# Turning z one pair before it is rounded, with a second buffer, in a fused attention and two-network kernel

## The chip, the core and the metric

The kernel runs on one core of a Trainium2 chip. The metric is the device time of one execution in microseconds (us), as a median over runs. Five engines have in-order queues of their own: TensorE (PE, with its weight loads as PEld), VectorE (DVE), ScalarE (ACT), GpSimd (POOL) and SyncE (SP, which here issues nearly all DMAs).

## The reference

```python
scores = matmul(z, z.T) / S          # z: (2, 3008, 64)
attn = maximum(scores, 0) ** 2
x = u * matmul(attn, v)              # u, v: (2, 3008, 256)
x = x.reshape(6016, 256)
h = x @ w_in1                        # w_in: (256, 2048), w_out: (2048, 256)
x = (h - tanh(h)) @ w_out1
h = x @ w_in2
g = where(h >= 1, h, where(h <= -1, 0, (h + 1) ** 2 / 4))
out = g @ w_out2
```

## The kernel before, in words

Each fp32 operand of a product is split in two rounded parts, `hi` (a ScalarE copy to the rounded type) and `lo` (VectorE: the operand less `hi`), and a product is three matmuls.

The program is one list of *pairs*, `pairs`. An attention pair is a batch b, a chunk c of 512 queries (six per batch, the last of 448) and two key tiles t of 128; there are twelve t. The first half of a pair, `attn_s`, makes the scores (six matmuls), the relu `r` (ScalarE, line 271), `hi` (line 274), the squares `a` (VectorE line 280; for every third t ScalarE line 278) and `lo` (VectorE, line 284, queued at the end of the pair). The second half, `attn_av`, accumulates `hi` and `lo` times v, and runs LAG = 2 pairs later. At a chunk's last pair two accumulators are added to `y` (lines 320, 321). A network pair is a chunk of 512 tokens and 256 hidden columns, done likewise (`ffn_s`, `ffn_av`, 24 matmuls). The score tiles and h have two PSUM buffers.

In the first chunk of each batch z (six tiles of 512 columns per batch), v (twelve) and, in the first chunk of each network, the weights (sixteen) are brought in *loads*. A load is a list of steps, each with the number of pairs by which it stands at the latest before its first use. The first is the DMA to a tile of the pool `raw` (six buffers), issued on SP's queue; then comes the work that puts the split operand into a ring of 18 tiles. For z the work is `turn` (VectorE transposes the raw tile into `zt`, line 126) and `cut` (ScalarE rounds `zt`, line 131; VectorE subtracts, line 132). For v and the weights it is a split (line 90 on ScalarE, line 93 on VectorE, where VectorE's part is put off to the next `flush`). `pump(i)` runs at the head of each pair i: it starts loads, does the steps that are due, and may do one more step ahead of time for a load whose last step lies two pairs back. Here `zt` has one buffer, and turn and cut of z are one step, `work`. A pool hands a buffer on in the order in which the program frees it.

The weights come as 8-byte numbers; a generator `convert` turns them with VectorE instructions spread over the attention pairs, and writes them back to memory. The pool `wide` (two buffers) holds their raw form. At the start, while the first DMAs are under way, `warm` runs matmuls on a tile `zero`.

Of the kernel before, what the change touches and what calls it, by code (L numbers as in the profile page):

```python
# [9 lines left out]
U32 = mybir.dt.uint32  # L10
BF16 = mybir.dt.bfloat16
# [4 lines left out]
P = 128  # L16
# [4 lines left out]
AHEAD = 14  # L21
# [6 lines left out]
def attention_then_two_ffn(  # L28
# [29 lines left out]
    const = ctx.enter_context(tc.tile_pool(name="const", bufs=1))  # L58
# [3 lines left out]
    wide_p = ctx.enter_context(tc.tile_pool(name="wide", bufs=2))  # L62
    raw_p = ctx.enter_context(tc.tile_pool(name="raw", bufs=6))
    u_p = ctx.enter_context(tc.tile_pool(name="u", bufs=2))
    zt_p = ctx.enter_context(tc.tile_pool(name="zt", bufs=1))
    tmp_p = ctx.enter_context(tc.tile_pool(name="tmp", bufs=2))
    sp_p = ctx.enter_context(tc.tile_pool(name="split", bufs=3))
    ps_s = ctx.enter_context(tc.tile_pool(name="ps_s", bufs=2, space=bass.MemoryType.PSUM))
# [9 lines left out]
    loads = []  # L78
    deferred = []

    def add_load(first, last, steps, slots=1):
        loads.append({"first": first, "last": last, "steps": steps[:2], "slots": slots, "parts": steps[2:]})

    def flush():
        for fn in deferred:
            fn()
        deferred.clear()
# [15 lines left out]
    def load_z(b, g):  # L103


        st = {}

        def dma(other=nc.sync):
            r = st["raw"] = raw_p.tile([P, QT], F32, tag="raw", name=f"zraw{b}_{g}")
            r3 = r.rearrange("p (c e) -> p c e", e=32)  # L110
            n = min(QT, S - QT * g) // 32
            for i in range(4):
                d = slice(32 * (i % 2), 32 * (i % 2) + 32)
                at = slice(32 * i, 32 * i + 32)
                (other if i % 2 else nc.sync).dma_start(
                    out=r3[at, :n, :],
                    in_=z[b, QT * g : QT * g + 32 * n, d].rearrange("(c a) e -> a c e", a=32),
                )
                if 32 * n < QT:
                    nc.sync.dma_start(  # L120
                        out=r3[at, n:, :], in_=z[b, S - REST :, d].rearrange("(c a) e -> a c e", a=32)
                    )

        def turn():
            st["zt"] = zt_p.tile([P, QT], F32, tag="zt", name=f"zt{b}_{g}")
            nc.vector.transpose(out=st["zt"], in_=st["raw"])  # L126

        def cut():
            zt = st["zt"]
            w = ring.tile([P, 2, QT], F32R, tag="w", name=f"z{b}_{g}")  # L130
            nc.scalar.activation(out=w[:, 0, :], in_=zt, func=AF.Copy, scale=ZEXP)
            nc.vector.scalar_tensor_tensor(
                out=w[:, 1, :], in0=zt, scalar=ZEXP, in1=w[:, 0, :].bitcast(F32), op0=ALU.mult, op1=ALU.subtract
            )
            zs[b, g] = w

        def work():
            turn()
            cut()

        return [(dma, AHEAD), (work, 2), turn, cut]

    def load_v(b, t):

# [309 lines left out]
    pairs = []  # L454
# [6 lines left out]
    for b in range(B):  # L461
        base = len(pairs)
        end = base + QC * NPA - 1
        lastc = base + (QC - 1) * NPA
        for t in range(NPA):
            if t % 2 == 0:
                g = t // 2

                add_load(base + t, end if g == QC - 1 else lastc + t + 1, load_z(b, g))
            add_load(base + t + LAG, lastc + t + LAG, load_v(b, t))  # L470
        for c in range(QC):
            p0 = len(pairs)
            for j in range(4):
                hook(p0 + UL + j, load_u, b, c, j)
            hook(p0 + UT, turn_u, b, c)
            for t in range(NPA):
                pairs.append((attn_s, attn_av, (b, c, t)))
    for net, (wi, wo) in enumerate(((w_in1, w_out1), (w_in2, w_out2))):
        base = len(pairs)
        for f in range(NPF):  # L480
            lastc = base + (NCH - 1) * NPF + f
            rows = slice(f * 2 * P, (f + 1) * 2 * P)
            cols = slice(f * 4 * P, (f + 1) * 4 * P)
            converts.append(convert((net, "in", f), wi[:, cols].rearrange("(k p) f -> p k f", p=P)))
            converts.append(convert((net, "out", f), wo[rows, :].rearrange("(k p) d -> p k d", p=P)))
            add_load(base + f, lastc, load_w((net, "in", f)))
            add_load(base + f + LAG, lastc + LAG, load_w((net, "out", f)))
        for c in range(NCH):
            hook(len(pairs) - 3, split_x, net, c)
            for f in range(NPF):  # L490
                pairs.append((ffn_s, ffn_av, (net, c, f)))

    zero = const.tile([P, 512], BF16, name="zero")

    def warm(n):

        ps = ps_a.tile([P, 512], F32, tag="acc", name="warm")
        for i in range(n):
            nc.tensor.matmul(ps, zero[:, :P], zero, start=True, stop=True)

    with tc.manual_schedule():
        nc.gpsimd.memset(zero, 0.0)

        live = []
        staged = []

        def advance(ld, i):
            ld["steps"].pop(0)[0]()
            ld["at"] = i
            if not ld["steps"]:  # L510
                staged.remove(ld)
                live.extend([ld["last"]] * ld["slots"])

        def pump(i):

            while loads and len(staged) < 4 and loads[0]["first"] <= i + AHEAD:
                ld = loads[0]
                free = RING - sum(x >= i - 1 for x in live) - sum(y["slots"] for y in staged)
                if free < ld["slots"]:
                    break  # L520
                loads.pop(0)
                staged.append(ld)
                advance(ld, i)
            n = 0
            for ld in list(staged):
                while ld in staged and ld["first"] - ld["steps"][0][1] <= i:
                    advance(ld, i)
                if i > 5 and ld in staged and ld["at"] < i - 1 and n < (i >= NATT or pairs[i][2][2] != 1):
                    advance(ld, i)
                    n += 1  # L530


        first = [loads.pop(0) for _ in range(4)]
        z0, v0, v1, z1 = first
        z0["steps"][0][0](nc.scalar)
        v0["steps"][0][0]()
        v1["steps"][0][0](nc.scalar)
        z1["steps"][0][0]()
        warm(WARM[0])
        z0["steps"][1][0]()  # L540
        v0["steps"][1][0]()
        flush()
        z1["parts"][0]()
        for ld in first:
            live.append(ld["last"])

        held = {}
        state = {"credit": 0.0, "step": 0}
        NATT = B * QC * NPA

        pauses = ((0, NPA), (NPA * QC - 9, NPA * QC + 13), (NATT - 5, NATT + 1))

        def make(i):

            if not any(a <= i < e for a, e in pauses):
                state["credit"] += CONVERT[0] if i < NATT else CONVERT[1]
            while converts and state["credit"] >= 1:
                state["credit"] -= 1
                state["step"] += 1
                if state["step"] == 1:  # L560
                    next(converts[0])
                elif state["step"] == 5 and len(converts) > 1:
                    next(converts[1])
                if next(converts[0], "end") == "end":
                    converts.pop(0)
                    state["step"] = 1

        def second(i):
            if i >= LAG:
                _, av_fn, args = pairs[i - LAG]  # L570
                av_fn(*args, *held.pop(i - LAG))

        def close():
            for fn in tail:
                fn()
            tail.clear()

        for i in range(len(pairs) + LAG):
            pump(i)
            for fn, args in hooks.get(i, ()):  # L580
                fn(*args)
            if i == LAG:
                second(i)
            if i < len(pairs):
                s_fn, _, args = pairs[i]
                held[i] = s_fn(*args)
            else:
                flush()
            if i == 0:
                close()  # L590
                z1["parts"][1]()
            elif i == 1:
                warm(WARM[1])
                close()
                v1["steps"][1][0]()
                flush()
            if i != LAG:
                second(i)
            make(i)
            close()  # L600
# [32 lines left out]
```

## Time and profile before

| what | value |
|---|---|
| median of 3 runs | 1536.03 us (1535.98 to 1537.39) |
| the profiled execution, its own time | 1536.36 us |
| its span in the trace | 1534.4 us |
| TensorE busy | 1519.9 us, 99% |
| VectorE busy | 1077.6 us, 70% |
| ScalarE busy | 818.9 us, 53% |

The span runs from the program's first instruction to its last; the execution's own time is 1.96 us longer. Every time stamp below is counted from the start of the span. Busy time of TensorE is modelled, and the matmuls are pipelined, so a late matmul is best seen by the distance of the starts. The attention lasts to about 500 us, the first network to about 1010 us.

### The profile page before, as it was taken

The numbers are of one execution on the slowest core, as the hardware profiler recorded it, in microseconds if no ns is written. First come the engines' busy times: TensorE is split into PE (matmuls) and PEld (weight loads), VectorE is DVE, ScalarE is ACT, GpSimd is POOL, SyncE is SP. The second block draws the span as 40 slices with busy tenths as digits, with TensorE's granted clock in tenths as the row PEclk, the third lists the DMA queues.
The fourth block names the chain that finished last, engine by engine and source line by source line (L and its number), as shares of the span: only waits on it lengthen the run. The fifth ranks groups of instructions, "written<-read, shape, count | busy, mean of one in ns | idle before, by whom it ended". The sixth has DMA issues, their size and how long they took to land.

```text
span 1534.4 us, 21242 instructions
## 1 busy us (share of the span) xinstructions
PE 1519.9 (99%) x8944; PEld 1264.8 (82%) x8944; DVE 1077.6 (70%) x1139; ACT 818.9 (53%) x866; POOL 0.7 (0%) x5
## 2 busy tenths in 40 slices
PE   9999999999999999999999999999999999999999
PEld 5788888888889888888888888897888888888888
DVE  7888887888888765666654444567767776777675
ACT  7777777877778544444444444454444444344443
POOL 0000000000000000000000000000000000000000
PEclk9999999999999999999999999999999999999999
DMA  6222143123224201110010000020000000000001
GB/s 136 65 56 56 49 102 66 32 56 80 53 56 109 76 21 41 42 41 25 25 49 0 0 1 1 14 55 14 1 14 14 15 14 15 14 14 4 11 15 25
DMA packets 146623, 56.69 MB, mean 37 GB/s; under 512 B 123616, under 2 KB 130144, under 8 KB 146528
## 3 DMA queue, kind: packets, MB, share of 16 engines
q1 hardware_dynamic: 145056, 54.81, 14.5%
q8 instruction: 70, 1.15, 0.3%
q10 hardware_dynamic: 1472, 0.52, 0.1%
q14 instruction: 25, 0.20, 0.0%
HBM read 40.76 MB, written 14.55 MB: 36 GB/s over the span
## 4 chain that ended last, share of the span: by engine, by line
PE 93%; DVE 4%; ACT 2%; issue 1%; DMA 1%; SPq 0%; DVEq 0%; ACTq 0%
PE acc L386 32%; PE acc L298 21%; PE h L355 11%; PE h L356 11%; PE h L354 11%; PE sc L263 5%; DVE a L280 1%; DVE lo L284 1%; PE acc L418 1%; ACT r L271 1%; DMA zraw<-in_z_dram 0%; DVE zt L126 0%; ACT hi L274 0%; DVE gl L93 0%; ACT a L278 0%
## 5 line engine op out<-in xcount | busy, mean ns | idle before, releaser
L386 PE MATMUL acc<-gh,w_out 128*128 128x512 f32 (+1 forms) x1472 | 360.3, 387 | 0.0
L90 ACT ACTIVATE gh<-g 128x1024 fp32r<-128x1024 f32 (+1 forms) x192 | 200.4, 1044 | 268.2 <-DVE g L373 142.5
L298 PE MATMUL acc<-hi,v 64*128 64x512 f32 (+1 forms) x2256 | 317.0, 385 | 5.4 <-DVE y L321 3.1
L386 PEld LDWEIGHTS acc<-gh,w_out 128*128 128x128 f32 x1472 | 275.5, 188 | 54.8
L355 PE MATMUL h<-xh,w_in 128*128 128x512 f32 (+1 forms) x768 | 295.7, 385 | 0.9 <-DVE w_in L93 0.7
L354 PE MATMUL h<-xl,w_in 128*128 128x512 f32 (+1 forms) x768 | 295.7, 385 | 0.0
L356 PE MATMUL h<-xh,w_in 128*128 128x512 f32 (+1 forms) x768 | 295.5, 385 | 0.0
L298 PEld LDWEIGHTS acc<-hi,v 64*128 64x128 f32 x2256 | 240.4, 184 | 52.0 <-DVE y L321 7.4
L93 DVE TENSOR_TENSOR gl<-g,gh 128x1024 fp32r<-128x1024 f32 (+1 forms) x192 | 230.0, 1198 | 68.6 <-ACT gh L90 68.6
L365 DVE TENSOR_TENSOR g<-h,t 128x1024 f32<-128x1024 f32 (+1 forms) x96 | 115.4, 1202 | 148.2 <-ACT t L363 148.2
L368 DVE TENSOR_SCALAR t<-h 128x1024 f32<-128x1024 f32 (+1 forms) x96 | 115.4, 1203 | 142.6 <-PE h L356 142.6
L284 DVE TENSOR_TENSOR lo<-a,hi 128x1024 fp32r<-128x1024 f32 (+1 forms) x144 | 172.7, 1200 | 53.7 <-ACT a L278 52.4
L386 PE MATMUL acc<-gl,w_out 128*128 128x512 f32 (+1 forms) x736 | 195.0, 387 | 0.0
L298 PE MATMUL acc<-lo,v 64*128 64x512 f32 (+1 forms) x1152 | 189.4, 384 | 1.7 <-DVE lo L284 1.5
L271 ACT ACTIVATE r<-sc 128x1024 f32<-128x1024 f32 (+1 forms) x144 | 144.9, 1006 | 85.6 <-PE sc L263 83.4
L371 ACT ACTIVATE t<-t 128x1024 f32<-128x1024 f32 (+1 forms) x96 | 100.3, 1044 | 156.8 <-DVE t L368 156.8
L363 ACT ACTIVATE t<-h 128x1024 f32<-128x1024 f32 (+1 forms) x96 | 96.9, 1009 | 160.8 <-PE h L356 160.7
L355 PEld LDWEIGHTS h<-xh,w_in 128*128 128x128 f32 x768 | 144.1, 188 | 29.6 <-DVE w_in L93 2.2
L354 PEld LDWEIGHTS h<-xl,w_in 128*128 128x128 f32 x768 | 144.2, 188 | 28.3 <-issue 0.9
L356 PEld LDWEIGHTS h<-xh,w_in 128*128 128x128 f32 x768 | 144.2, 188 | 27.6
L386 PEld LDWEIGHTS acc<-gl,w_out 128*128 128x128 f32 x736 | 137.8, 188 | 27.5
L298 PEld LDWEIGHTS acc<-lo,v 64*128 64x128 f32 x1152 | 137.2, 184 | 22.9 <-DVE lo L284 3.8
(54 smaller groups left out, 1098.2 us busy)
## 6 DMA issues: line engine op xcount, KB each, us to landing
wide_in<-in_moe_w_in_dram SPq DMA_DIRECT2D x16, 512.0 KB, 4.2
wide_out<-in_moe_w_out_dram SPq DMA_DIRECT2D x16, 512.0 KB, 3.9
out_dram<-ot SPq DMA_DIRECT2D x88, 64.0 KB, 1.9
vraw<-in_v_dram SPq DMA_DIRECT2D x21, 256.0 KB, 3.1
ub<-in_u_dram SPq DMA_DIRECT2D x80, 64.0 KB, 2.7
w_in<-m_in SPq DMA_DIRECT2D x16, 256.0 KB, 2.2
w_out<-m_out SPq DMA_DIRECT2D x16, 256.0 KB, 2.2
wraw_in<-w_in SPq DMA_DIRECT2D x16, 256.0 KB, 2.8
```

The costliest lines, as they stand in the source:

```text
L90: nc.scalar.activation(out=hi, in_=src, func=AF.Copy)
L93: nc.vector.tensor_tensor(out=lo, in0=src, in1=hi.bitcast(F32), op=ALU.subtract)
L271: nc.scalar.activation(out=r[s], in_=ps[s], func=AF.Relu)
L284: tail.append(lambda: nc.vector.tensor_tensor(out=lo[s], in0=a[s], in1=hi.bitcast(F32)[s], op=ALU.subtract))
L298: nc.tensor.matmul(acc[d][h][:, :n], lhsT, g[half, j, :n], start=start, stop=stop)
L354: nc.tensor.matmul(ps[:, j, :n], w[:, 0, k, fs], xl[:, k, :n], start=(k == 0), stop=False)
L355: nc.tensor.matmul(ps[:, j, :n], w[:, 1, k, fs], xh[:, k, :n], start=False, stop=False)
L356: nc.tensor.matmul(ps[:, j, :n], w[:, 0, k, fs], xh[:, k, :n], start=False, stop=(k == 1))
L365: nc.vector.tensor_tensor(out=g[s], in0=ps[s], in1=t1[s], op=ALU.subtract)
L368: nc.vector.tensor_scalar(out=t1[s], in0=ps[s], scalar1=1.0, scalar2=-1.0, op0=ALU.min, op1=ALU.max)
L371: nc.scalar.activation(out=t1[s], in_=t1[s], func=AF.Square, scale=0.5, bias=0.5)
L386: nc.tensor.matmul(acc[d][:, :n], w[:, part, j, d * P : (d + 1) * P], g[:, j, :n], start=start, stop=stop)
```

## The change

The pool `zt` gets a second buffer. A load of z now has three steps: DMA, `turn` (due three pairs ahead of its first use) and `cut` (two ahead), so that the two are done in different pairs. In the networks `pump` may do two steps ahead of time per pair where it did one. The tile `zero` moves from a pool of its own into a buffer of `wide`. The calls at the start follow the new form of the steps and do the same work in the same order.

```diff
-    zt_p = ctx.enter_context(tc.tile_pool(name="zt", bufs=1))
+    zt_p = ctx.enter_context(tc.tile_pool(name="zt", bufs=2))
...
-        loads.append({"first": first, "last": last, "steps": steps[:2], "slots": slots, "parts": steps[2:]})
+        loads.append({"first": first, "last": last, "steps": steps, "slots": slots})
...
-        def work():
-            turn()
-            cut()
-
-        return [(dma, AHEAD), (work, 2), turn, cut]
+        return [(dma, AHEAD), (turn, 3), (cut, 2)]
...
-    zero = const.tile([P, 512], BF16, name="zero")
+    zero = wide_p.tile([P, 1024], U32, tag="wide", name="zero").bitcast(BF16)[:, :512]
...
-                if i > 5 and ld in staged and ld["at"] < i - 1 and n < (i >= NATT or pairs[i][2][2] != 1):
+                if i > 5 and ld in staged and ld["at"] < i - 1 and n < (2 if i >= NATT else pairs[i][2][2] != 1):
...
         z0["steps"][1][0]()
+        z0["steps"][2][0]()
         v0["steps"][1][0]()
         flush()
-        z1["parts"][0]()
+        z1["steps"][1][0]()
...
-                z1["parts"][1]()
+                z1["steps"][2][0]()
```

VectorE's queue at the start of the first chunk, before; in a name the first number is that of the z or v tile:

```order
L132 SCALAR_TENSOR_TENSOR z_1_168<-zt_1_140,z_1_168 128x512
L280 TENSOR_TENSOR a<-r 128x1024
L284 TENSOR_TENSOR lo<-a,hi 128x1024
L93 TENSOR_TENSOR v_1_192<-vraw_1_113,v_1_192 128x512
L126 STREAM_TRANSPOSE zt_2_197<-zraw_2_146 128x512
L132 SCALAR_TENSOR_TENSOR z_2_199<-zt_2_197,z_2_199 128x512
L93 TENSOR_TENSOR v_2_195<-vraw_2_142,v_2_195 128x512
L284 TENSOR_TENSOR lo<-a,hi 128x1024
L280 TENSOR_TENSOR a<-r 128x1024
L93 TENSOR_TENSOR v_3_253<-vraw_3_144,v_3_253 128x512
L284 TENSOR_TENSOR lo<-a,hi 128x1024
```

The same place of VectorE's queue after the change (lines stand four lower in the file):

```order
L132 SCALAR_TENSOR_TENSOR z_1_168<-zt_1_140,z_1_168 128x512
L126 STREAM_TRANSPOSE zt_2_171<-zraw_2_146 128x512
L276 TENSOR_TENSOR a<-r 128x1024
L280 TENSOR_TENSOR lo<-a,hi 128x1024
L93 TENSOR_TENSOR v_1_194<-vraw_1_113,v_1_194 128x512
L132 SCALAR_TENSOR_TENSOR z_2_199<-zt_2_171,z_2_199 128x512
L93 TENSOR_TENSOR v_2_197<-vraw_2_142,v_2_197 128x512
L280 TENSOR_TENSOR lo<-a,hi 128x1024
L126 STREAM_TRANSPOSE zt_3_255<-zraw_3_248 128x512
L276 TENSOR_TENSOR a<-r 128x1024
L93 TENSOR_TENSOR v_3_253<-vraw_3_144,v_3_253 128x512
L280 TENSOR_TENSOR lo<-a,hi 128x1024
```

The turn of z2 has moved ahead of a pair's `a` and `lo` and of v1's subtraction, and that of z3 has come up from below these rows; the subtractions of z stand where they stood.

ScalarE's queue around the change of batch, before; names begin with batch and tile, `z1_2` is the third z tile of the second batch:

```order
L131 ACTIVATE z1_2_3263<-zt1_2_3261 128x512
L271 ACTIVATE r_3276<-sc_3266 128x2x448
L274 ACTIVATE hi_3274<-r_3276 128x2x448
L278 ACTIVATE a_3273<-r_3276 128x2x448
L90 ACTIVATE v1_4_3307<-vraw1_4_3165 128x512
L271 ACTIVATE r_3319<-sc_3309 128x1024
L274 ACTIVATE hi_3317<-r_3319 128x1024
L271 ACTIVATE r_3361<-sc_3351 128x1024
L320 ACTIVATE y_3364<-acc00_2851 128x448
L320 ACTIVATE y_3364<-acc10_2853 128x448
L274 ACTIVATE hi_3359<-r_3361 128x1024
L90 ACTIVATE v1_5_3391<-vraw1_5_3209 128x512
```

And after:

```order
L131 ACTIVATE z1_1_3248<-zt1_1_3160 128x512
L267 ACTIVATE r_3261<-sc_3251 128x2x448
L270 ACTIVATE hi_3259<-r_3261 128x2x448
L274 ACTIVATE a_3258<-r_3261 128x2x448
L90 ACTIVATE v1_3_3292<-vraw1_3_3111 128x512
L267 ACTIVATE r_3304<-sc_3294 128x1024
L270 ACTIVATE hi_3302<-r_3304 128x1024
L267 ACTIVATE r_3351<-sc_3341 128x1024
L316 ACTIVATE y_3354<-acc00_2851 128x448
L316 ACTIVATE y_3354<-acc10_2853 128x448
L270 ACTIVATE hi_3349<-r_3351 128x1024
L131 ACTIVATE z1_2_3381<-zt1_2_3339 128x512
```

At the same pairs ScalarE is one z and one v behind where it was: z1_2 is now rounded after the copies of `y`, and v1_4 and v1_5 follow it.

VectorE's queue in the second network, before; `w1_in_7` is the last of its first-layer weights:

```order
L93 TENSOR_TENSOR w1_in_6_10199<-wraw1_in_6_10114,w1_in_6_10199 128x512
L93 TENSOR_TENSOR xl1_1_10202<-x1_91,xh1_1_10201 128x1024
L373 TENSOR_TENSOR g_10218<-h_10204,t1_10217 128x1024
L368 TENSOR_SCALAR t1_10257<-h_10244 128x1024
L93 TENSOR_TENSOR gl_10220<-g_10218,gh_10219 128x1024
L93 TENSOR_TENSOR w1_out_6_10240<-wraw1_out_6_10153,w1_out_6_10240 128x512
L93 TENSOR_TENSOR w1_in_7_10242<-wraw1_in_7_10195,w1_in_7_10242 128x512
```

And after:

```order
L93 TENSOR_TENSOR w1_in_7_10205<-wraw1_in_7_10124,w1_in_7_10205 128x512
L93 TENSOR_TENSOR xl1_1_10208<-x1_91,xh1_1_10207 128x1024
L369 TENSOR_TENSOR g_10224<-h_10210,t1_10223 128x1024
L364 TENSOR_SCALAR t1_10261<-h_10248 128x1024
L93 TENSOR_TENSOR gl_10226<-g_10224,gh_10225 128x1024
```

The split of `w1_in_7` stands in the pair in which that of `w1_in_6` stood.

## Rows read from the trace of the kernel before

**Rows 1.** The page: the span, and part 1, busy time by engine.

```profile
span 1534.4 us, 21242 instructions
...
PE 1519.9 (99%) x8944; PEld 1264.8 (82%) x8944; DVE 1077.6 (70%) x1139; ACT 818.9 (53%) x866; POOL 0.7 (0%) x5
```

**Rows 2.** Chain that ended last, in time: start us, us, what.

```profile
58.73 3.01 PE acc L298 x23
62.42 2.72 PE acc L298 x24
...
99.39 3.01 PE acc L298 x23
...
263.06 3.02 PE acc L298 x23
...
305.02 3.01 PE acc L298 x23
...
511.71 2.72 PE acc L386 x12
```

**Rows 3.** Waits, whole span: who waited for whom, us in total, times, longest.

```profile
ACT z L131 <- DVE zt L126: 25.4, 11, 3.7
...
DVE zt L126 <- DMA zraw<-in_z_dram: 4.3, 2, 4.1
...
PEld h L355 <- DVE w_in L93: 2.2, 3, 1.1
```

**Rows 4.** Timeline of ScalarE: start us, us, instruction, idle before and its releaser.

```profile
21.48 0.61 ACT L90 ACTIVATE v<-vraw 128x512 fp32r<-128x512 f32 x1
24.13 0.63 ACT L131 ACTIVATE z<-zt 128x512 fp32r<-128x512 f32 x1 [2.04 <-DVE zt L126]
24.67 1.00 ACT L271 ACTIVATE r<-sc 128x1024 f32<-128x1024 f32 x1
```

**Rows 5.** Timeline of VectorE, first chunk.

```profile
11.65 1.22 DVE L280 TENSOR_TENSOR a<-r 128x1024 f32<-128x1024 f32 x1
...
14.12 0.69 DVE L93 TENSOR_TENSOR v<-vraw,v 128x512 fp32r<-128x512 f32 x1
...
23.39 0.70 DVE L126 STREAM_TRANSPOSE zt<-zraw 128x512 f32<-128x512 f32 x1
```

**Rows 6.** Timeline of TensorE, first chunk.

```profile
1.31 4.85 PE L499 MATMUL warm<-zero 128*128 128x512 bf16 x11 [1.31 <-POOL zero L502]
...
9.26 2.11 PE L298 MATMUL acc<-hi,v 64*128 64x512 f32 x16 [0.34 <-ACT hi L274]
...
14.86 1.67 PE L298 MATMUL acc<-hi,v 64*128 64x512 f32 x12 [0.67 <-DVE v L93]
...
25.72 0.96 PE L263 MATMUL sc<-z,z 64*128 64x512 f32 x6 [0.74 <-ACT r L271]
```

**Rows 7.** Busy by stretch: length, PE, PEld, DVE, ACT, POOL, granted clock, DMA.

```profile
21.39:53.64 32.25, 30.23 (x242) 21.66 (x240) 26.80 (x33) 26.13 (x34) 0.00 (x0) 1.00 0.45 108
```

**Rows 8.** Timeline of SP's queue: the issue of z3's DMAs.

```profile
14.83 3.37 SPq L115 DMA_DIRECT2D zraw<-in_z_dram  x4
```

**Rows 9.** Line 115, z's DMAs, in the first 60 us.

```profile
DMA to landing us min/median/max: 1.9/2.6/4.9
```

**Rows 10.** Waits of TensorE from 250 to 310 us.

```profile
PE acc L298 <- DVE y L321: 2.0, 2, 1.7
PE acc L298 <- DVE lo L284: 1.5, 2, 1.1
PE acc L298 <- ACT y L320: 0.4, 1, 0.4
PE sc L263 <- ACT r L271: 0.4, 1, 0.4
```

**Rows 11.** Timeline of TensorE, second network.

```profile
1049.19 0.39 PE L354 MATMUL h<-xl,w_in 128*128 128x512 f32 x1
1050.28 0.50 PE L355 MATMUL h<-xh,w_in 128*128 128x512 f32 x1 [0.71 <-DVE w_in L93]
```

## The prediction

> **What bounds the kernel now.** I read the page first: TensorE is busy for 1519.9 of 1534.4 us [rows 1], so only the time in which its queue stands still can be won, and the question is where that is. The chain in order of time answers it [rows 2]. In a settled attention chunk 24 accumulate matmuls take 2.72 us, two of half height side by side, so one takes 0.113 us; with six for the scores a pair is 30 matmuls, 3.40 us. A whole chunk is 99.39 - 58.73 = 40.66 us. Two chunks are longer, the first of each batch, in which z and v are loaded. The second of these lasts 305.02 - 263.06 = 41.96 us, and the change of batch stands ahead of it. The networks run at 2.72 us for 12 matmuls, 0.227 each.
>
> Then the waits of all engines [rows 3]: ScalarE stood 25.4 us in 11 places at line 131, the rounding of z, until VectorE had turned the tile. No other row names z with so much. What that does to TensorE is seen in one place. ScalarE ends a v at 21.48 + 0.61, has nothing to do until the turn that VectorE starts at 23.39 is over, rounds z at 24.13 and only then takes the relu r at 24.67 [rows 4, 5]. TensorE's next scores need the PSUM tile that this r empties, and start at 25.72 after 0.74 us of idleness [rows 6]. VectorE was late with the turn because it stands behind `lo`, which itself waits for ScalarE: the two engines wait for each other by turns, and TensorE for both.
>
> **The change part by part.** No instruction is added or dropped; the work of every engine stays, its order moves.
>
> *First chunk.* From the first accumulate matmul at 9.26 to the mark at 58.73 are 49.47 us [rows 2, 6]. The like stretch of a settled chunk is 40.66 us, and 0.68 us (six score matmuls) more because two pairs of scores are issued ahead at the start. The excess is 49.47 - 41.34 = 8.13 us. What stays of it: TensorE's wait for v1 before 14.86, 0.67 us, and the slow start behind it (12 matmuls in 1.67 us, where 12 x 0.113 is 1.36), 0.31 us. What is added: the turn of z2 now stands ahead of the squaring `a` that began at 11.65 and so ahead of v1's subtraction, which was 14.12 [rows 5]. A turn lasts 0.70 us and the next instruction follows some 0.1 us before its end (14.12 to 14.72 for a v of 0.69), so v1 and the matmuls that wait for it come 0.60 us later. All other stalls of this stretch hang on z's rounding: with z2 to z5 turned in the pair before, ScalarE finds each ready. At the place above it could round z at 22.09 instead of 24.13, r would end near 23.6, and TensorE, which got there 0.74 us before 25.72, would not wait, with 1.3 us in hand. So the first term is 8.13 - 0.67 - 0.31 - 0.60 = **6.55 us**. Its bounds: 8.13 if v1 were hidden as well, and 4.4 if a third of the stalls came back.
>
> Does VectorE keep up if TensorE no longer waits? In 32.25 us of this chunk, in which it made nine `lo`, VectorE was busy 26.80 and ScalarE 26.13 us [rows 7]. Nine pairs at 3.40 are 30.6 us, so both would be at 85 to 88%. That is the cover under which the moved instructions cost nothing; were it gone, each turn (0.60) and its subtraction (0.60) would lie open, 1.2 us per z.
>
> Do the loads keep up? A turn now stands behind nothing that takes long, but everything of VectorE stands behind it: `a`, v's subtraction and `lo` of the pair, for which TensorE waits. For z3 the four DMAs went out from 14.83 in 3.37 us [rows 8], the last about half a microsecond before 18.20. DMAs of this line land 1.9 to 4.9 us after issue, 2.6 in the middle [rows 9], so z3 lay ready near 20.3, 3.1 us before its turn at 23.39; a pair is 3.40. Moved by one pair alone the turn would be at the edge. But the raw buffers are handed on in the order in which the program frees them. Now the turn of z2 stands ahead of v1's work, so z3's DMAs get z2's buffer, free at about 11.65 + 0.70 = 12.35, and not v1's, free at 14.12 + 0.69 = 14.81. They can start 2.5 us sooner. I take no wait; the bound is the 3.4 us of a pair once.
>
> *Change of batch.* From 250 to 310 us TensorE stood still in six waits of 4.3 us together: y 2.0, `lo` 1.5, r 0.4, y's copy 0.4 [rows 10]; all follow within a few pairs on a rounding of z that waited up to 3.7 us [rows 3]. The chunk from 263.06 is 1.30 us longer than a settled one, of which 0.7 are in these waits (the shorter y and `lo`, 0.3 and 0.4); 0.6 more makes 4.9. I leave the 0.3 of a y, since the sum of two accumulators at a chunk's end has to wait for TensorE anyhow. Second term **4.6 us**, bounds 2.5 (the long y and the second `lo` stay: 4.6 - 1.7 - 0.4) and 5.9 (4.3 with 0.1 to 0.2 of slow start at each wait, and 0.6). Here each z goes through three steps and not two, so z0's rounding and v1 to v4 come up to one pair later than before, still ahead of their first use.
>
> *Networks.* At the start of the second network three weight loads waited 2.2 us for the subtraction of `w_in`, the longest 1.1 [rows 3]. For TensorE the longest cost 1050.28 - 1049.19 - 0.23 = 0.86 us [rows 11], 0.27 less than the weights' wait; two of 0.55 then cost 0.28 each, in all 1.4, and 1.5 with slow starts. Two splits in a pair bring the last `w_in` one pair, 24 x 0.227 = 5.44 us, forward; the wait was at most 1.1. Third term **1.5 us**, bounds 0 and 2.2. The cover: two splits cost VectorE 1.2 us in 5.44.
>
> *The zero tile* shares a buffer with the wide loads; the warm matmuls are done long before the second of these. Nothing.
>
> The sum is 6.55 + 4.6 + 1.5 = 12.65 us. The profiled execution took 1536.36 us (span 1534.4 and 1.96 around it), 0.33 above the median of 1536.03; so 1523.7 for it and **1523.4 us** for the median.
>
> **The rivals.**
>
> *Part of it only:* the batch change or the networks keep their stalls, or a load is late for a turn or two. For it: the batch change moves v behind z, and in the waits two turns did stand for a DMA, 4.3 us [rows 3]; against it: those were the first two, before any buffer was in use. Without the second term 1528.0, with two turns late by a pair, 3.40 us each, 1530.2.
>
> *The change doesn't do what it says:* ScalarE finds z ready, but its r then waits for scores, since TensorE was held by v or `lo`, and the stalls come back elsewhere. It would need VectorE as the bound, and that has 12% left. Time 1533 to 1538.
>
> *Slower:* in-order blocking on VectorE. If loads land more than a pair later than I reckon, each of the ten later turns stands for its DMA with `a` and `lo` of the pair behind it. The point from which it decides: a load later than the 3 us that z3 had over, by 1.6 us at each of ten turns, gives back 16 us: 1539.4. Against it the earlier buffers.
>
> *The clock falls:* TensorE's wait for v1 grows from 0.67 to 1.27 us. [...] Before 263.06 TensorE idled 1.7 us [rows 10], and 23 matmuls, two side by side, followed in 3.02 us as in other chunks [rows 2]: no fall. [...]
>
> **How the numbers follow.** Forecast 76 in 100, part of it 13, no effect 6, slower 3, the clock 2. The forecast's own range is 1521.4 (6.55, 5.9 and 2.2 give 14.65) to 1526 (a little over half of the second term lost). To leave out no more than two in ten, the range reaches 0.6 below it, for a third of v1's wait being hidden, and to the first of the partial cases: 1520.8 to 1528.4. A difference under 0.2%, 3.1 us, can't be told from none; faster by more is the forecast, the clock, the partial cases and a little of "no effect": 0.92; within 0.2% 0.05; slower 0.03.
>
> **What would show it.** Right: the wait of line 131 for the turn falls from 25.4 us to a few; the stretch from the first accumulate matmul to the next chunk's mark is near 43 us and not 49.47; TensorE's wait for v1 is longer by 0.6; no wait of `w_in` near the second network's start. Wrong: VectorE's turn waits for `zraw` in more than the first two places, or the waits for `lo` and y at the change of batch stay.

## The result and the profile after

The changed kernel takes 1521.48 us (median of 4 executions, 1521.3 to 1521.72), the kernel before beside it 1536.61 (4 executions, 1535.98 to 1537.39): a ratio of 0.9899, 95% interval 0.9887 to 0.991. The forecast was 1523.4 with a range from 1520.8 to 1528.4.

The page of the changed kernel, span and part 1, answers to [rows 1]:

```profile
span 1519.7 us, 21264 instructions
...
PE 1512.9 (100%) x8944; PEld 1268.5 (83%) x8944; DVE 1076.6 (71%) x1139; ACT 819.6 (54%) x866; POOL 0.7 (0%) x5
```

The counts are what they were on every engine, and so is the busy time of VectorE and ScalarE to within 1 us; the span is 14.7 us shorter. TensorE's modelled busy time fell too, from 1519.9 to 1512.9 us with the same 8944 matmuls, so half of the gain stood in the rows of before as slow matmuls and not as idleness. The waits of the whole span answer to [rows 3]:

```profile
PEld acc L294 <- DVE y L317: 4.6, 11, 0.7
DVE zt L126 <- DMA zraw<-in_z_dram: 4.1, 1, 4.1
...
ACT z L131 <- DVE zt L126: 1.3, 1, 1.3
...
PE acc L294 <- DVE v L93: 0.9, 1, 0.9
```

ScalarE's wait for a turned z fell from 25.4 us in 11 places to 1.3 in one. VectorE's turn waits for a DMA once, at the start, so the loads keep up. No weight load waits for `w_in` any more. TensorE's wait for v1 is longer, 0.9 us where it was 0.67 [rows 6].

The chain in order of time answers to [rows 2] (start us, us, what):

```profile
92.89 3.02 PE acc L294 x23
...
252.04 3.03 PE acc L294 x23
...
292.73 3.02 PE acc L294 x23
```

Each line is the start of a chunk. Against the same marks of before the first is 99.39 - 92.89 = 6.50 us earlier, the last 305.02 - 292.73 = 12.29. The chunk from 252.04 is 292.73 - 252.04 = 40.69 us long, as a settled one; it was 41.96.

The first pairs on TensorE (start us, us, instruction, idle before and releaser):

```profile
9.59 2.14 PE L294 MATMUL acc<-hi,v 64*128 64x512 f32 x16 [0.34 <-ACT hi L270]
...
15.35 1.66 PE L294 MATMUL acc<-hi,v 64*128 64x512 f32 x12 [0.90 <-DVE v L93]
```

The wait for v1 ends at 15.35 where it ended at 14.86, and from there to the chunk's end TensorE's timeline shows no idle. ScalarE at the same time:

```profile
19.00 0.61 ACT L90 ACTIVATE v<-vraw 128x512 fp32r<-128x512 f32 x1
19.52 0.62 ACT L131 ACTIVATE z<-zt 128x512 fp32r<-128x512 f32 x1
20.04 1.00 ACT L267 ACTIVATE r<-sc 128x1024 f32<-128x1024 f32 x1
```

v, z and r follow one another without the 2.04 us of [rows 4]. VectorE's timeline, for [rows 5]:

```profile
11.55 0.70 DVE L126 STREAM_TRANSPOSE zt<-zraw 128x512 f32<-128x512 f32 x1
12.18 1.18 DVE L276 TENSOR_TENSOR a<-r 128x1024 f32<-128x1024 f32 x1
...
14.61 0.68 DVE L93 TENSOR_TENSOR v<-vraw,v 128x512 fp32r<-128x512 f32 x1
```

SP's issue of z3's DMAs, which stood at 14.83 for 3.37 us [rows 8]:

```profile
12.29 1.92 SPq L115 DMA_DIRECT2D zraw<-in_z_dram  x4
```

The turn of z2 now stands ahead of `a`, v1's subtraction moved from 14.12 to 14.61, and z3's DMAs go out 2.5 us sooner, at the moment z2's turn lets its raw buffer go.

To see where the time came from, the start of the same matmul (the k-th of 8944) was compared in the two traces. The gain is 6.5 us at the end of the first chunk, 12.3 at 307 us, 12.9 from 501 us until 1037 us, and 14.7 from 1051 us, early in the second network, to the end. So the first chunk gave 6.5, the change of batch 5.8, the last chunk (448 queries) of the second batch 0.6, the networks 1.8. The first accumulate matmul stands 0.33 us later than before (9.59 and 9.26), ahead of the first moved instruction, z2's turn at 11.55; counted from there the first chunk gave 6.83.

### The profile page after: what moved, and what is told of

It reads as the page before. It is cut to its first block, busy times and chain, and to the rows that moved or that the text cites. A ratio compares the mean times of both kernels' runs of the same rounds, so it can differ in the third digit from the quotient of the medians.

```text
span 1519.7 us, 21264 instructions
## 1 busy us (share of the span) xinstructions
PE 1512.9 (100%) x8944; PEld 1268.5 (83%) x8944; DVE 1076.6 (71%) x1139; ACT 819.6 (54%) x866; POOL 0.7 (0%) x5
## 4 chain that ended last, share of the span: by engine, by line
PE 98%; DVE 1%; SPq 0%; ACT 0%; issue 0%; DMA 0%; DVEq 0%; ACTq 0%
PE acc L382 33%; PE acc L294 25%; PE h L350 11%; PE h L352 11%; PE h L351 11%; PE sc L259 6%; PE acc L414 1%; SPq L115 0%; SPq L147 0%; DVE a L276 0%; DMA zraw<-in_z_dram 0%; DVE lo L280 0%; ACT r L267 0%; DVE gl L93 0%; DVE g L369 0%
## 5 line engine op out<-in xcount | busy, mean ns | idle before, releaser
L294 PE MATMUL acc<-hi,v 64*128 64x512 f32 (+1 forms) x2256 | 310.7, 384 | 1.8 <-DVE v L93 0.9
L267 ACT ACTIVATE r<-sc 128x1024 f32<-128x1024 f32 (+1 forms) x144 | 145.2, 1008 | 95.5 <-PE sc L259 93.4
L294 PE MATMUL acc<-lo,v 64*128 64x512 f32 (+1 forms) x1152 | 184.5, 382 | 0.0
L270 ACT ACTIVATE hi<-r 128x1024 fp32r<-128x1024 f32 (+1 forms) x144 | 150.3, 1044 | 4.2
```

The source lines that it names most:

```text
L267: nc.scalar.activation(out=r[s], in_=ps[s], func=AF.Relu)
L270: nc.scalar.activation(out=hi[s], in_=r[s], func=AF.Square)
L294: nc.tensor.matmul(acc[d][h][:, :n], lhsT, g[half, j, :n], start=start, stop=stop)
```

## The experiments

The theory: each of the three places earns its own saving, because a z's turn and its rounding stand in different pairs, so that no engine waits for the other within a pair. Rivals: the buffer or the earlier moment does it; the savings are not separate, since one place uncovers the stall of another.

**One part at a time.** In the first, `pump` does one step ahead per pair in the networks again, as below; the second is the kernel before with this line alone changed the other way.

```diff
-                if i > 5 and ld in staged and ld["at"] < i - 1 and n < (2 if i >= NATT else pairs[i][2][2] != 1):
+                if i > 5 and ld in staged and ld["at"] < i - 1 and n < (i >= NATT or pairs[i][2][2] != 1):
```

> The turn of z one pair ahead of its rounding, with two buffers, but one split ahead of time per pair in the networks as before. Theory (order): the terms are independent, so all is kept but the third, which by the starts of the matmuls is 1.7 us: 1523.2 us, with the three w_in waits of 2.2 us back near the second network's start. Rival (the gain came mostly from the networks): above 1530.

> The kernel before with nothing but two splits ahead of time per pair in the networks. Theory: 1.7 us faster than before, so 1534.4 to 1535, and no w_in wait near the second network's start; the waits of line 131 stay at 25 us. Rival (the w_in waits lie in slack, or two splits in a pair press VectorE into new waits): no difference, 1536 to 1536.6.

Without the networks' part 1523.59 us (1523.39 to 1523.88; ratio to before 0.991, 0.9897 to 0.9924), 2.1 over the full change. With that part alone 1535.69 against 1537.33 of the kernel before beside it, 1.6 less (0.9989, 0.998 to 0.9998). In both traces the starts of the matmuls differ by 1.8 us in the networks, as between the two kernels themselves, and without the networks' part the three waits for `w_in` are back with 2.2 us.

In the next two, the z tiles of one batch are turned and rounded in one step again, those of batch 1 as below, those of batch 0 with the condition `b == 0 and g > 1` (tiles 0 and 1 have calls of their own at the start and are left):

```diff
+        def work():
+            turn()
+            cut()
+
+        if b == 1:
+            return [(dma, AHEAD), (work, 2)]
         return [(dma, AHEAD), (turn, 3), (cut, 2)]
```

> The changed kernel, but the z tiles of batch 1 are turned and rounded in one step again; those of batch 0 and the networks stay as changed. Theory (each place earns its own saving, and the time's scatter of some 2 us in the kernel before comes from the clock falling in the wait at the change of batch): the first chunk's 6.5 us and the networks' 1.8 us stay, the change of batch gives its 5.8 us back, 1527.3 us, with a granted clock of 1.000 in some executions, and up to 2 us more, 1529.3 us, with 0.999 in others; the wait of the first accumulate of batch 1 for y is back at some 1.7 us. Rival (the scatter has another place): all executions within 0.6 us of each other. Rival (the stretch at the change of batch was shortened by something else than the z tiles): 1521.5 us.

> The changed kernel, but the z tiles 2 and on of batch 0 are turned and rounded in one step again; batch 1 and the networks stay as changed. Theory: the first chunk gives its 6.5 us back and nothing else changes, 1528.0 us, granted clock 1.000 and a scatter under 0.6 us, since the long wait at the change of batch stays away. Rival (what is saved in the first chunk is partly lost to a later wait that it uncovers): nearer to 1525 than to 1528 us. Rival (the scatter comes from the first chunk's waits): the granted clock is 0.999 in some executions, and those are some 2 us longer.

With batch 1 in one step 1527.88 us (1527.76 to 1528.53; 0.9943, 0.993 to 0.9957), with batch 0 in one step 1528.33 (1528.2 to 1528.65; 0.9945, 0.993 to 0.9961). They give back 6.4 and 6.85 us. By the starts of the same matmuls in the traces, each gave back at its own place what that place had earned: with batch 0 in one step 6.3 us by the end of the first chunk and nothing more up to 460 us, with batch 1 in one step 5.7 us at the change of batch, and without the networks' part 1.8 in the networks. So the savings are separate. The sum of the execution times, 6.4 + 6.85 + 2.1 = 15.35, also meets the 15.3 by which the kernel before beside them (1536.75) stood over the changed one, but by luck: each of the three runs took 0.4 to 0.6 us longer in the last chunk of the second batch (below), which the sum counts three times; and 1536.75 is the median of executions with and without a fall of the clock (below). The scatter of up to 2 us that was expected of the first of them did not show in its four executions, although the wait for y was back with 1.73 us; a further run is given below.

**Buffer, moment, or separation.** The changed kernel with one buffer for `zt`; the kernel before with two buffers, the new place of `zero` and nothing else; and this last with the undivided work one pair earlier (the first pair of lines is the edit of the first kernel, the second that of the last):

```diff
-    zt_p = ctx.enter_context(tc.tile_pool(name="zt", bufs=2))
+    zt_p = ctx.enter_context(tc.tile_pool(name="zt", bufs=1))
...
-        return [(dma, AHEAD), (work, 2), (turn, 0), (cut, 0)]
+        return [(dma, AHEAD), (work, 3), (turn, 0), (cut, 0)]
```

> The changed kernel with one zt buffer and not two. Theory (order): the turn of the next z stands behind the rounding and the subtraction of the one before in program order in every case but at the very start, so the second buffer is not needed: 1521.5 within 0.3 us. Rival (the buffer does it): the turn waits for the tile's last reader again, and most of the 15 us comes back: above 1530.

> Two zt buffers and the zero tile in wide, but turn and rounding in one step as before, and one split ahead of time in the networks. Theory (order): ScalarE still arrives at the rounding before VectorE has come to the turn, 25 us in 11 waits, and the time is that of before, 1536 to 1536.6. Rival (the buffer does it): 1523 to 1528.

> Turn and rounding of z in one step as before, but this step one pair earlier (three pairs ahead of the first use), with two zt buffers; networks as before. Theory (order between the engines): what counts is that other work stands between turn and rounding; together they make ScalarE wait for the turn as before, only a pair earlier, so no gain, 1535 to 1539, and the waits of line 131 stay above 20 us. Rival (being early is what counts): 1523 to 1526.

One buffer: 1521.83 us (0.9898, 0.9885 to 0.9912), within 0.35 us of two. Buffers alone: 1537.55 (1.0001, 0.9992 to 1.001). Earlier, but together: 1537.94 (1.0006, 0.9997 to 1.0015). ScalarE's wait for a turned z in the three, in this order:

```profile
ACT z L131 <- DVE zt L126: 1.5, 1, 1.5
ACT z L131 <- DVE zt L126: 25.0, 11, 3.7
ACT z L131 <- DVE zt L126: 26.6, 11, 3.8
```

For z it is the separation alone: the wait goes with it and stays without it, whatever the buffers and the moment. All 11 executions of the last kernel lie above 1537.7, and its profile shows the clock at 0.51 from 264 to 266 us, behind the wait for y; less the 1.6 us that such a fall costs (below) it still gains nothing. The turn of one pair finds `zt` free because the rounding and the subtraction of the pair before have read it.

**How far apart.** The turn another pair ahead, as below; and turn and rounding both one pair later, with (turn, 2) and (cut, 1):

```diff
-        return [(dma, AHEAD), (turn, 3), (cut, 2)]
+        return [(dma, AHEAD), (turn, 4), (cut, 2)]
```

> The changed kernel with the turn due four pairs ahead and not three, so two pairs ahead of the rounding. Theory (in-order VectorE): at the start the turn of z2 comes before its DMAs have landed and stands with a, lo and v1 behind it for 2 to 3 us, so TensorE waits longer before the first lo or v1: 1523 to 1525, slower than the changed kernel. Rival (the more ahead the better): 1521 or less.

> The changed kernel with the turn due two pairs ahead and the rounding one pair ahead: still one pair apart, but each a pair later. Theory: the order between the engines is kept and z2's turn no longer stands ahead of v1's subtraction (0.6 us back), but z comes close to its use and a few scores wait for it (under 1 us): 1521 to 1522.3. Rival (z has to be early): 1525 or more.

Two ahead: 1526.16 us (1524.55 to 1526.19; 0.9925, 0.9913 to 0.9938), 4.7 slower than the change, in the expected direction but by more. VectorE's timeline in that kernel:

```profile
11.43 0.71 DVE L126 STREAM_TRANSPOSE zt<-zraw 128x512 f32<-128x512 f32 x1 [2.93 <-DMA zraw<-in_z_dram]
12.06 1.18 DVE L276 TENSOR_TENSOR a<-r 128x1024 f32<-128x1024 f32 x1
13.35 1.23 DVE L280 TENSOR_TENSOR lo<-a,hi 128x1024 fp32r<-128x1024 f32 x1
```

And TensorE's:

```profile
14.63 2.07 PE L294 MATMUL acc<-lo,v 64*128 64x512 f32 x8 [2.85 <-DVE lo L280]
16.50 2.76 PE L259 MATMUL sc<-z,z 64*128 64x512 f32 x12
19.06 2.72 PE L294 MATMUL acc<-hi,v 64*128 64x512 f32 x16
```

Here is the rival of in-order blocking, at one turn: it waits 2.93 us for its DMA, `a` and `lo` stand behind it, and TensorE waits 2.85 for `lo`. Twelve score matmuls then take 2.76 us, 1.52 in the changed kernel. The stretch behind (length, PE, PEld, DVE, ACT, POOL, granted clock, DMA share, GB/s):

```profile
16.00:18.00 2.00, 2.00 (x12) 1.53 (x10) 1.90 (x3) 0.00 (x0) 0.00 (x0) 0.50 0.00 0
18.00:20.00 2.00, 2.00 (x12) 1.51 (x12) 1.45 (x3) 1.94 (x2) 0.00 (x0) 0.50 0.24 60
```

Behind 2.85 us of idleness TensorE's granted clock is 0.50 in both stretches, with 12 matmuls in 2 us; the changed kernel has 21 and 20 from 16 to 18 and from 18 to 20 us, at a clock of 1.00. So the 4.7 us are the blocking and a fall of the clock together: of the five executions the one with a mean clock of 1.000 is the fastest, 1524.55, 3.1 over the change.

Both later: 1522.55 us (1522.16 to 1523.09; 0.9906, 0.9892 to 0.9919), 1.1 slower than the change and a little over what was expected. The step of one pair between the two counts for most; the moment for 1 us at most, of which the trace puts 0.4 in the last chunk of the second batch, where the edit does nothing (below).

**The wait that was left.** v1's split issued with pair 0 and not with pair 1, to hide the 0.90 us:

```diff
             if i == 0:
...
                 z1["steps"][2][0]()
+                v1["steps"][1][0]()
+                flush()
             elif i == 1:
...
-                v1["steps"][1][0]()
-                flush()
```

> The changed kernel with v1's split issued in the first pair, ahead of z2's turn and of the second pair's squares. Theory: TensorE's wait for v1, 0.9 us idle and 1.3 us by the starts, is the last large one at the start; it goes, at a price of half a microsecond at most for a later relu of the second pair: 1520.0 to 1520.8. Rival (something else, the relu or lo, is late next at the same place): 1521.5.

1521.51 us (1520.89 to 1521.56; 0.9898, 0.9884 to 0.9911): no gain. TensorE's timeline shows the wait gone, all 16 matmuls in one row with no idle before it:

```profile
13.53 1.98 PE L294 MATMUL acc<-hi,v 64*128 64x512 f32 x16
```

Matmul for matmul it is 1.4 us ahead of the changed kernel by the third pair, 0.8 at the end of the first chunk and 0.2 at the end. Half a microsecond of this is lost in the last chunk of the second batch, whose length differs between kernels for no reason that this edit gives (below). The 0.6 in the first chunk is lost in two places: 0.2 at 34 us, and the rest around a wait of 0.18 us for y at the chunk's end. At the first, VectorE's timeline and that of the weight loads show:

```profile
32.16 0.71 DVE L126 STREAM_TRANSPOSE zt<-zraw 128x512 f32<-128x512 f32 x1 [1.66 <-issue]
34.64 1.23 PEld L294 LDWEIGHTS acc<-hi,v 64*128 64x128 f32 x12 [0.36 <-DVE v L93]
```

The turn of the last z of batch 0 begins after 1.66 us of idleness, and v's subtraction stands behind it. The profile names no releaser; the last of this tile's DMAs was issued at 28.67 us and z's DMAs landed 1.6 to 4.8 us after issue (28.75 us, and 1.7 to 4.8, in the changed kernel), so a late load is likely, but not shown. The rival was near in its time, then, but not in its place. No version ran faster than the change.

**The scatter of the kernel before.** Its 60 executions in these comparisons lie between 1535.58 and 1538.2 us; the 18 with a mean granted clock of 1.000 reach up to 1536.75, and all 32 above 1537 show 0.997 to 0.999, as do ten of those below. The profile of one of its relatives (the networks' part alone) fell on such an execution. TensorE's timeline at the change of batch in it:

```profile
262.87 3.16 PE L298 MATMUL acc<-hi,v 64*128 64x512 f32 x15 [1.73 <-DVE y L321]
265.41 2.06 PE L298 MATMUL acc<-lo,v 64*128 64x512 f32 x8
```

The same place in the kernel before:

```profile
263.06 2.11 PE L298 MATMUL acc<-hi,v 64*128 64x512 f32 x15 [1.73 <-DVE y L321]
264.79 1.28 PE L298 MATMUL acc<-lo,v 64*128 64x512 f32 x8
```

And the stretch behind the wait (columns as above, the granted clock third from the end), first in that kernel:

```profile
264.00:266.00 2.00, 2.00 (x12) 1.53 (x12) 2.00 (x3) 1.46 (x2) 0.00 (x0) 0.50 0.00 0
```

Then in the kernel before as profiled:

```profile
264.00:266.00 2.00, 2.00 (x22) 1.70 (x20) 2.00 (x3) 1.66 (x2) 0.00 (x0) 1.00 0.00 0
```

The same wait of 1.73 us, the same instructions, and 12 matmuls against 22 in 2 us: the clock fell in one execution and not in the other. By the starts of the same matmuls the fall cost 1.6 us. Two runs test whether that wait is the cause. One fills it, in the kernel before, with matmuls of zeros into the accumulator that is about to be started afresh:

```diff
             accs[b, c] = [[ps_a.tile([P, 512], F32, tag="acc", name=f"acc{d}{h}") for h in range(2)] for d in range(2)]
+            for _ in range(6 if b == 1 and c == 0 else 0):
+                nc.tensor.matmul(accs[b, c][0][0], zero[:, :P], zero, start=True, stop=True)
```

> The kernel before, with six matmuls of zeros (128x512, some 0.2 us each) put ahead of the first accumulate of batch 1, into the accumulator that this accumulate then starts afresh; they fall into the 1.73 us in which TensorE waits for y there. Nothing else changes. Theory (idle time of TensorE at this place lets the granted clock fall in some executions): with the idle time cut to some 0.4 us the clock falls more seldom, and the median comes down from 1537.3 to near 1536.2 us; executions that still show 0.999 are those in which it falls a pair earlier, behind the 1.1 us wait for lo. Rival (the clock falls by chance, whatever TensorE does): median 1537.3 us and as many executions of 0.999 as the kernel before has.

The other keeps the wait in the changed kernel: batch 1 in one step, as above, and one step ahead per pair in the networks.

> The changed kernel with the z tiles of batch 1 in one step again, and one load a pair in the networks again: what is left of the change is the z tiles of batch 0. In more executions than the four with batch 1 alone in one step. Theory (each place earns its own): 6.5 us under the kernel before where both keep the clock, 1529.6 us. Two readings of the scatter: if the 1.73 us wait for y is enough by itself to let the granted clock fall in about half of the executions, as in the kernel before, about half of these stand near 1531.3 us with a clock under 1.000, and the median is between 1529.6 and 1531.3 us; if it is not enough (it is the whole of what TensorE did since the start that decides, so that a kernel whose first chunk is 6.5 us shorter comes to the wait at another moment), all stand within 0.8 us of 1529.6 us.

With the wait filled 1536.25 us, and all 11 executions between 1535.71 and 1536.46, where the kernel before beside it went from 1535.58 to 1537.85 (median 1536.75; ratio 0.9995, 0.9987 to 1.0004). TensorE there:

```profile
260.87 1.46 PE L291 MATMUL acc<-zero 128*128 128x512 bf16 x6 [0.35 <-ACT y L322]
262.25 0.50 PE L300 MATMUL acc<-hi,v 64*128 64x512 f32 x1
263.10 1.20 PE L300 MATMUL acc<-hi,v 64*128 64x512 f32 x8 [0.34 <-DVE y L323]
```

The accumulate still starts at 263.1, so no work was saved; only the longer executions are gone. Four of the 11 still show a mean clock of 0.999, and are no longer than the rest (1535.88 to 1536.31 us): a mean under 1.000 does not by itself make an execution longer. None of the four was profiled, but the profile of the buffers alone (1535.88 us at 0.999) shows such a fall, one pair earlier:

```profile
257.84 1.06 PE L298 MATMUL acc<-lo,v 64*128 64x448 f32 x4 [1.10 <-DVE lo L284]
262.81 2.13 PE L298 MATMUL acc<-hi,v 64*128 64x512 f32 x15 [0.80 <-DVE y L321]
260.00:262.00 2.00, 2.00 (x13) 1.34 (x9) 2.00 (x2) 1.73 (x4) 0.00 (x0) 0.66 0.41 97
```

The clock fell behind the 1.10 us wait for `lo`, the slower matmuls used up part of the wait for y, 0.80 where it was 1.73, and the accumulate started at 262.81, no later than elsewhere. With the wait kept: 1529.64 and 1530.0 us at a clock of 1.000, and 1531.14, 1531.62 and 1531.71 at 0.999 (median 1531.14; 0.996, 0.9946 to 0.9974). By clock and time it fell in three of five, as the first reading had it. Its profile is one of the latter:

```profile
257.00:259.00 2.00, 2.00 (x12) 1.58 (x14) 2.00 (x3) 1.97 (x3) 0.00 (x0) 0.57 0.10 15
259.00:261.00 2.00, 2.00 (x14) 1.58 (x12) 2.00 (x3) 0.51 (x1) 0.00 (x0) 0.58 0.00 0
```

So the idle time at the change of batch lets the clock fall in some executions, and costs them 1.1 to 2.1 us more, 1.6 by the starts of the matmuls in this trace. The executions of 1529.64 and 1530.0 also give the first chunk's worth alone: 6.2 to 6.6 us under the 1536.2 that is the middle of the 18 executions of before with a full clock.

## Why the prediction was right

**The sum.** Of 12.65 us forecast the traces show 14.7. The difference is 1.2 at the change of batch, 0.3 in the networks and 0.6 that was not foreseen; the first chunk fits.

**The bound.** Counting TensorE's lost time by the starts of its matmuls was right. The prediction's first sentence was not: by it at most the 1534.4 - 1519.9 = 14.5 us of idleness could be won, yet 14.7 went and 6.8 us of idleness are left, since slow matmuls behind the waits count as busy. The rival "the change doesn't do what it says" is out. ScalarE's `r` does wait longer for scores, 93.4 us where it was 83.4, but TensorE is not held: its own waits fell from 9.8 us to 2.8, and none is for `lo`.

**The cover.** The 85 to 88% worked out from [rows 7] were a misreading. That stretch holds nine `lo`, but 242 matmuls, which are eight pairs of 30 and not nine; eight pairs at 3.40 are 27.2 us, and 26.80 and 26.13 us in them are 99 and 96%. After the change the same number of matmuls, and of VectorE's and ScalarE's instructions, stands in (columns as above):

```profile
17.77:44.97 27.20, 27.20 (x242) 22.48 (x240) 26.48 (x33) 25.94 (x34) 0.00 (x0) 1.00 0.56 130
```

VectorE is busy 97% of it, ScalarE 95%. So VectorE did not have the 12% left on which the prediction put that rival aside, but 3%. That this was enough is measured, and was luck in the prediction.

**First chunk, 6.55.** Measured 6.50 by the marks; taken back alone 6.85, of which the trace puts 6.3 here and 0.6 in the last chunk. The stretch that was to fall from 49.47 to near 43 is 92.89 - 40.66 - 9.59 = 42.64 us. One small part was too large: v1 was to come 0.60 later, and came 0.49 later, but 0.33 of that stood already at the first accumulate, so the moved turn cost some 0.2. z3's raw buffer came from z2, as argued, 2.5 us sooner. The rival of blocking by late loads had its condition right: a turn placed another pair ahead does block, and costs 4.7 us, 3.1 where the clock stayed up. This change stays clear of it by less than a pair: before the turn at 30.76 us, that of the last z of batch 0, VectorE stands idle 0.18 us, with no releaser named.

**Change of batch, 4.6.** The mechanism was right, the size 1.2 us short: 5.79 by the marks; taken back alone 6.4, of which the trace puts 5.7 here and 0.6 in the last chunk. The step that mis-sized it is "The chunk from 263.06 is 1.30 us longer than a settled one, of which 0.7 are in these waits (the shorter y and `lo`, 0.3 and 0.4); 0.6 more makes 4.9". It priced the slow starts behind the two waits after 263.06 and gave the four ahead of it none. Matmul for matmul the wait of 1.09 us for `lo` cost 1.5: ten matmuls around it lasted 2.6 us before (255.49 to 258.09) and 1.1 after (247.92 to 249.03). Of the 4.3 us of waits 0.32 stayed, for y at 252.04; so of 5.8 some 4.0 are waits and 1.8 restarts.

**Networks, 1.5.** Measured 1.8 in the traces, 1.6 and 2.1 in the single parts; inside its bounds. By the starts of the matmuls the two short waits gave 0.4 each, not 0.28, and the longest 1.0, not 0.86. The zero tile: nothing to be seen in the buffers alone, which include it.

**The clock.** That the wait for v1 would not lower it was right, in part by luck: the wait came to 0.90 us and not to the 1.27 forecast, and behind 1.10 us, in the buffers alone, the clock did fall (0.66 from 260 to 262 us). The argument for it was weak. The prediction took from [rows 2, 10] that a wait of 1.7 us had left the clock alone. It had in that one execution; judged by their times it had not in 32 of the 60 others. The forecast gave a fall at the wait for v1 a chance of 2 in 100 and counted it among the faster outcomes; no row of before shows what such a fall costs. The two falls priced by the starts above cost 1.6 us each. The same wait of 1.73 us ended at a granted clock of 1.00 in one trace and of 0.50 in another; why was not tested. So the median of before used as the base, 1536.03 of three, lies among the executions with a full clock, and the middle of all 60 is 1537.1: against that the change gains a further microsecond, with the wait for y down from 1.73 us to 0.32 and the clock at 1.000 in all four executions.

**Not foreseen: 0.6 us in a chunk of 448 queries.** The last chunk of the second batch, the same 295 matmuls, in the kernel before (columns as above):

```profile
467.33:497.90 30.57, 30.57 (x295) 29.08 (x293) 26.88 (x36) 26.79 (x33) 0.00 (x0) 1.00 0.50 136
```

And in the changed one:

```profile
455.04:485.02 29.98, 29.98 (x295) 27.47 (x293) 26.56 (x35) 26.76 (x33) 0.00 (x0) 1.00 0.50 139
```

TensorE is never idle in either, at the same clock. The timelines differ in one thing: before, score and accumulate matmuls of the two half-height streams interleave one by one, after, they keep in step. In the other traces the chunk takes one of three lengths. The longest, 30.6 us, also ran with the networks' part alone, with either batch in one step, with the wait for y filled and with v1 first. One of 30.35 ran with the buffers alone, without the networks' part, with the first chunk alone and with both steps later. The shortest ran with one buffer, with the turn two ahead, and with turn and rounding earlier but together. That last kernel has nothing of the separation, so the change does not set the length directly; what does is open.

## What to carry to other kernels

When one engine hands a tile to another within one step, put the two halves into different steps of the schedule before adding buffers: the separation earned the whole of the gain at the z tiles, the second buffer none. Put a step only so early that its DMA has landed, because everything behind it in that engine's queue waits with it, as `a` and `lo` did here for 2.93 us. Price a stall of TensorE by the distance of starts, not by the idle shown (1.5 us and 1.09 for one `lo` here), and look at several executions before you say that a wait leaves its clock alone (behind the 1.73 us for y here it was 1.00 in one trace and 0.50 in another).

## What the runs showed of the hardware

- TensorE's granted clock fell to 0.50 behind an idle of 1.73 us in the trace of the networks' part alone and stayed at 1.00 in that of the kernel before, with the same instructions at that place. It fell behind 1.10 us in the trace of the buffers alone (0.66 from 260 to 262 us) and behind 2.85 us in that of the turn two ahead (0.50 from 16 to 20 us); behind 0.90 us the mean stayed at 1.000 in all of the four executions of the changed kernel. A fall behind the wait for y cost 1.1 to 2.1 us, 1.6 in two traces; the one behind 1.10 us cost nothing, as the next wait, 0.80 us where it was 1.73, took the delay up.
- Six matmuls of zeros in that wait took the longer executions away: none of 11 was above 1537 us, where 7 of 15 of the kernel before beside it were, with nothing else changed.
- In the last chunk of the second batch the two half-height matmul streams of 448 columns ran a pair, behind the chunk's first, in 3.04 us in the changed kernel, where they keep in step, and in 3.04 to 3.10 in the kernel before, where they interleave: the same 295 matmuls took 29.98 and 30.57 us, and 30.35 in other runs.
